# State products in column tiles, words scaled on VectorE, a row-tiled selection, and new durations for the planner

## The chip, the cores and the metric

One core of a Trainium2 chip runs the whole program. The metric is the device time of one execution in microseconds (us), the median of the runs shown. The engines are named as in the profile: PE (TensorE matmul), PEld (its weight load), DVE (VectorE), ACT (ScalarE), POOL (GpSimd) and SP (SyncE, which issues nearly all transfers in one queue).

## The reference, cut to what matters

```python
# 1. gated linear attention, B=4 H=8 S=768 D=48
scale = np.minimum(mag, 0.999) / (mag + 1e-06)            # mag = |a_re + i a_im|
for t in range(S):
    S_re, S_im = ar*S_re - ai*S_im + k_t v_t, ar*S_im + ai*S_re
    y[:, :, t] = einsum('bhd,bhde->bhe', q[:, :, t], S_re)
x = y.transpose(0, 2, 1, 3).reshape(3072, 384)
# 2. soft mixture of experts: 32 slots, 8 experts, 384 -> 1024 -> 384
d = softmax(x @ phi, axis=0);  slot_input = d.T @ x
slot_out[e] = relu(slot_input[e] @ w1[e]) @ w2[e]
x = softmax(x @ phi, axis=1) @ slot_out
# 3. feed-forward, 384 -> 2048 -> 384
g = np.maximum(0.01 * h, h)                               # h = x @ w_in
return g @ w_out
```

The arrays `w_in` and `w_out` of the feed-forward reach the kernel as 64-bit floats, which it turns into 32-bit floats itself.

## The kernel before, in words

**Attention.** The sequence is cut into 6 chunks of 128 steps, and each chunk into two units of 16 heads, so there are 12 units u = 0 to 11, of 128 x 768 values each. For a unit, `prep1`, `modulus`, `excess`, `logs` and `prep2` take the logarithm and the angle of the gates; `phase` and `decay` sum them along time with a triangular matmul (L562); `prep3` makes cosine and sine; `prep4` scales q and k (L619) and spreads them over the two (L628). Then `attend` works in four groups of four heads: `mA` transposes q and k (L643, copied out at L647 or L649), `mB` multiplies them (L658) and masks the result (L661, DVE), `mC` makes the output (L683), `mD` makes the state for the next chunk, and `mE` transposes the output (L721, L725, L728). The state product of `mD` (L700) takes, for each of 8 heads of a half unit, a 128 x 96 weight (k times cosine and sine) and 48 columns of v; it is made for the first ten units, two halves each, so 20 times. Its result is added to the old state and decayed (L710, L712, L713). After every second unit `slots` adds the chunk to the 32 slots of the mixture.

**64-bit words.** `narrow` turns 128 x 384 words of 64 bits into 32-bit floats: `ACT` takes the absolute value of the high words (L439), DVE bounds it from below (L440), shifts the mantissa (L441), puts in the sign (L442) and the low bits (L443). `conv_wi` does so for 16 pieces of `w_in` during attention, and `conv_wo` for 16 pieces of `w_out` around the start of the feed-forward, where it also splits the result in two (L471, L472).

**Experts and feed-forward.** `layer1` and `layer2` multiply the 32 slots with all expert weights: 64 slabs of 384 KB each, which stream in as buffers come free (`load_slabs`). `output` transposes the result, and `product` multiplies it with `w_in` (L1014). One 128-row tile holds four groups of 32 rows there; each group is picked out by a 128 x 128 matrix of zeros and ones, `sel`, which `select` builds, and lands in a tile `gs` (L1022, L1023). From there on `ffn1` (L1039, then L1041 to L1043) and `ffn2` (L1056 to L1058, 1152 matmuls of 384 columns in all) fill the rest of the program, and L1066 stores the output.

**What sets the order.** Nothing is issued as it is written. Every operation is given to `Plan` with an estimated duration; `Plan.emit` computes from these how late each may start (`backward`) and then fills each engine in turn (`forward`), taking the time at which a loaded tile is there from `delay`. The order that results is fixed in the program: each engine, and the transfer queue of SP, goes through its own list and waits at an instruction until what it needs is there. Buffers come from pools (`Tag`); the largest, `w`, has 33 tiles of 384 KB that gates, q, k, v, raw words and slabs share. The durations are numbers in the code, for example:

```python
pe(1.36, mm, ks + [v], [b])                        # mD, L702
cost = max(0.45, 0.06 + nbytes / 0.36e6)           # a transfer of SP, L110
return 0.0 if not o.bytes else 4.0 if o.eng == "POOL" else 2.0   # delay, L144
```

Of the kernel before, what the change touches and what calls it, by code (L numbers as in the profile page):

```python
# [42 lines left out]
EARLY, LATE = {9: 2, 10: 4, 11: 8}, (18,)  # L43
# [53 lines left out]
class Plan:  # L97
# [222 lines left out]
def tile_kernel(  # L320
# [316 lines left out]
    def mA(u, hq):  # L637
        for nm, tg in (("q", t_qt), ("k", t_kt)):
# [13 lines left out]
    def mB(u, hq):  # L652
        b, t = b_sc(), t_sc([P, 4, P])
# [10 lines left out]
    def mC(u):  # L664

# [68 lines left out]
    def slots(c):  # L734

        nonlocal phi_mm, ms_mm
        last = c == NCH - 1
# [429 lines left out]
```

## Time and profile before

| | |
|---|---|
| median of 3 runs | 502.66 us (502.05 to 502.67) |
| profiled execution | 502.35 us, span 500.6 us |
| instructions | 10447 |
| busy: PE, PEld, DVE, ACT, POOL | 485.2, 440.0, 318.6, 356.5, 18.2 us |
| chain of work that ended last | PE 70%, DVE 15%, ACT 8%, DMA 5% |
| moved by DMA | 67.09 MB, mean 134 GB/s |

The span runs from the first to the last instruction of the program; 1.75 us of the execution lie around it. The busy time of PE is an upper bound of its work, since matmuls overlap. A mean over the whole span hides that the program has stages: attention to about 234 us, the expert layers to about 274 us, and the feed-forward to the end. So the windows, which give busy time by stretch, are read beside the chain. In the rows, a 32-bit matmul counts as two instructions.

### The profile page before, as it was taken

Reading aid. Unit: us, or ns where it says so; the run is one execution under the profiler, and the core shown is the slowest. Engines: PE = TensorE matmul, PEld = TensorE weight load, DVE = VectorE, ACT = ScalarE, POOL = GpSimd, SP = SyncE. Lnnn points to the kernel's source line nnn. Section 1 sums busy time; section 2 is a strip of 40 time slices with the busy share of each in tenths; the row PEclk is TensorE's granted clock in tenths of the full one; section 3 lists DMA queues with packets and bytes.
Section 4 is the critical chain, followed back from the end, with each engine's and each line's share of the span. In section 5 each row is a group of like instructions: output and inputs, shape, how many; then the busy total and the mean of one; then the engine's idle time right before and its main releaser. Section 6 shows DMA issues by size and latency. Waiting matters only on the chain.

```text
span 500.6 us, 10447 instructions
## 1 busy us (share of the span) xinstructions
PE 485.2 (97%) x4066; PEld 440.0 (88%) x4066; DVE 318.6 (64%) x669; ACT 356.5 (71%) x684; POOL 18.2 (4%) x37
## 2 busy tenths in 40 slices
PE   8797999999999999999999999999999999999997
PEld 8675779979979988889545999999999999999996
DVE  3767899999999998986535999334500542035300
ACT  7998999999999999944215998079802993079502
POOL 1010002001001000001000000000000000000000
PEclk9999999999999999999999999999999999999999
DMA  8987344465677393599899221011000010010002
GB/s 300 324 196 234 98 129 147 109 192 142 181 221 217 75 260 118 191 323 318 286 395 352 64 64 33 0 48 48 2 0 33 17 48 1 0 48 16 33 1 94
DMA packets 46890, 67.09 MB, mean 134 GB/s; under 512 B 22004, under 2 KB 28132, under 8 KB 46840
## 3 DMA queue, kind: packets, MB, share of 16 engines
q1 hardware_dynamic: 46088, 65.99, 41.4%
q8 instruction: 32, 0.52, 0.4%
q10 hardware_dynamic: 432, 0.39, 0.2%
q0 software_dynamic: 320, 0.03, 0.1%
q14 instruction: 18, 0.15, 0.1%
HBM read 61.59 MB, written 4.81 MB: 133 GB/s over the span
## 4 chain that ended last, share of the span: by engine, by line
PE 70%; DVE 15%; ACT 8%; DMA 5%; issue 1%; SPq 0%; ACTq 0%; DVEq 0%
PE b L1056 13%; PE b L1058 13%; PE b L1057 13%; PE bm L683 5%; PE bsc L658 5%; PE b L1039 4%; PE btr L643 4%; PE bc L562 3%; PE bsc L700 3%; DMA w<-in_w_dram 2%; DVE w L619 2%; DVE sc L661 2%; DMA w<-in_wo_dram 2%; DVE q L628 2%; DVE k L628 1%; PE b L934 1%
## 5 line engine op out<-in xcount | busy, mean ns | idle before, releaser
L1043 DVE TENSOR_TENSOR w<-x,w 128x384 fp32r<-128x384 f32 x128 | 69.0, 555 | 104.6 <-ACT w L1042 103.8
L1056 PE MATMUL b<-w 128*128 128x384 f32 x384 | 128.5, 335 | 0.0
L1058 PE MATMUL b<-w 128*128 128x384 f32 x384 | 128.3, 334 | 0.0
L1057 PE MATMUL b<-w 128*128 128x384 f32 x384 | 128.3, 334 | 0.0
L1056 PEld LDWEIGHTS b<-w 128*128 128x128 f32 x384 | 72.1, 188 | 0.3 <-ACT x L1041 0.2
L1057 PEld LDWEIGHTS b<-w 128*128 128x128 f32 x384 | 72.1, 188 | 0.0
L1058 PEld LDWEIGHTS b<-w 128*128 128x128 f32 x384 | 72.1, 188 | 0.0
L1065 ACT ACTIVATE k<-b 128x384 f32<-128x384 f32 x24 | 11.4, 488 | 79.1 <-PE b L1058 78.9
L1042 ACT ACTIVATE w<-x 128x384 fp32r<-128x384 f32 x128 | 63.4, 525 | 4.9 <-PE b L1058 3.2
L1041 ACT ACTIVATE x<-b 128x384 f32<-128x384 f32 x128 | 59.9, 487 | 2.4 <-PE b L1039 1.5
L658 PE MATMUL bsc<-qt,kt 96*128 96x128 f32 x384 | 50.8, 278 | 0.4 <-DVE S L710 0.2
L658 PEld LDWEIGHTS bsc<-qt,kt 96*128 96x128 f32 x384 | 46.4, 192 | 2.1 <-DVE S L710 0.5
L661 DVE TENSOR_TENSOR sc<-bsc,tri_r 128x512 f32<-128x512 f32 x48 | 32.5, 684 | 7.3 <-PE bsc L658 6.9
L683 PE MATMUL bm<-sc,w 128*64 128x128 f32 (+1 forms) x384 | 35.5, 275 | 0.0
L649 ACT ACTIVATE qt<-btr 96x512 f32<-96x512 f32 x48 | 28.4, 591 | 9.2 <-PE btr L643 9.1
L186 ACT ACT_TABLE_LOAD x25 | 32.1, 1283 | 2.6 <-issue 2.2
L643 PE MATMUL btr<-ident,k 128*96 128x128 f32 x192 | 29.3, 275 | 2.4 <-ACT kt L649 1.7
L683 PE MATMUL bm<-qt,S 96*48 96x128 f32 x320 | 31.1, 272 | 0.0
L700 PEld LDWEIGHTS bsc<-w,k 128*96 128x96 f32 x320 | 28.9, 165 | 2.0 <-issue 1.0
L643 PE MATMUL btr<-ident,q 128*96 128x128 f32 x192 | 29.5, 276 | 1.2 <-DVE kt L647 0.6
L700 PE MATMUL bsc<-w,k 128*96 128x48 f32 x320 | 29.6, 247 | 0.3 <-PE bm L771 0.3
L643 PEld LDWEIGHTS btr<-ident,q 128*96 128x96 f32 x192 | 21.0, 127 | 6.2 <-issue 1.7
(179 smaller groups left out, 798.2 us busy)
## 6 DMA issues: line engine op xcount, KB each, us to landing
w<-in_w_dram SPq DMA_DIRECT2D x50, 384.0 KB, 6.1
w<-in_qkv_dram SPq DMA_DIRECT2D x36, 384.0 KB, 5.9
w<-in_a_dram SPq DMA_DIRECT2D x22, 384.0 KB, 4.2
w<-in_wi_dram SPq DMA_DIRECT2D x16, 384.0 KB, 4.2
w<-in_wo_dram SPq DMA_DIRECT2D x16, 384.0 KB, 5.5
out_dram<-k SPq DMA_DIRECT2D x24, 192.0 KB, 1.9
cs<-in_w_dram SPq DMA_DIRECT2D x4, 384.0 KB
k<-in_w_dram SPq DMA_DIRECT2D x6, 192.0 KB, 3.7
```

Source lines behind the costliest of these rows:

```text
L186: self.preload(TABLES[name])
L643: T.transpose(b()[:96, P * i:P * i + P], src()[:, i].rearrange("p t d -> p (t d)"), ident)
L658: T.matmul(b()[:, P * i:P * i + P], lhsT=k()[:96, i, :], rhs=q()[:96, i, :], start=True, stop=True)
L661: dve(c_dve(512), lambda: V.tensor_tensor(t(), b().rearrange("p (i t) -> p i t", t=P), tri.unsqueeze(1).to_broadcast([P, 4, P]), op=ALU.mu ...
L683: T.matmul(y()[64 * j:64 * j + m, o:o + P], lhsT=l, rhs=r, start=kind == 0, stop=kind == 1 or c == 0)
L700: T.matmul(b()[:96, D * i:D * i + D], lhsT=ks[i // 4]()[:, i % 4].rearrange("p t d -> p (t d)"), rhs=v()[:, D * g:D * g + D], start=True, ...
L1041: act(NG, lambda: A.activation(u(), b()[:, :NG], AF.Prelu, alpha=0.01), [b], [u])
L1042: act(NG, lambda: A.activation(g()[:, 0], u(), AF.Copy), [u], [(g, 0)])
L1043: dve(c_dve(NG), lambda: V.tensor_tensor(g()[:, 1], u(), g()[:, 0].bitcast(F32), op=ALU.subtract), [u, (g, 0)], [(g, 1)])
L1056: T.matmul(b()[:, :DM], lhsT=lh, rhs=wh()[:, i], start=f == FO[0], stop=False)
L1057: T.matmul(b()[:, :DM], lhsT=ll, rhs=wh()[:, i], start=False, stop=False)
L1058: T.matmul(b()[:, :DM], lhsT=lh, rhs=wl()[:, i], start=False, stop=f == FO[-1])
```

## The change

Four places of the work are changed, and numbers of the planner.

1. `mD`: each 128 x 96 weight is cut into three of 32 columns, which write to partitions 0, 32 and 64 of the output. There are 24 matmuls for 8.
2. `narrow`: the instruction on ACT and the bound are gone. DVE multiplies the high words by 2^-112 (it reads every second 32-bit word for that), shifts, and puts in sign and low bits as before; it has four instructions as before.
3. `select` and `product`: `sel` is one 128 x 128 tile for each half, built by 2 instructions in place of 5; the four groups are matmuls over 32 rows each.
4. `Plan`: durations in some twenty places, the time of a transfer, and the time until a large transfer has landed (4.0 us where it was 2.0). The order in which operations are given to the planner is written out as a string, `PROGRAM`; the same steps stand there in the same order as in the loop before. `LEADS` is empty.

```diff
-        act(n, lambda: A.activation(t1(), hi().bitcast(F32), AF.Abs), [raw], [k1])
-        dve(c_dve2(n), lambda: V.tensor_scalar(t1(), t1(), 2.0 ** -15, None, op0=ALU.max), [], [k1])
-        dve(c_dve2(n), lambda: V.tensor_scalar(i0(), i1(), 0x07FFFFFF, 3, op0=ALU.bitwise_and, op1=ALU.logical_shift_left), [k1], [k0])
-        dve(c_dve(n), lambda: V.scalar_tensor_tensor(i0(), hi(), -0x40000000, i0(), op0=ALU.bitwise_and, op1=ALU.bitwise_or), [raw], [k0])
+        dve(c_dve2(n), lambda: V.tensor_scalar(t1(), hi().bitcast(F32), 2.0 ** -112, None, op0=ALU.mult), [raw], [k1])
+        dve(c_dve2(n), lambda: V.tensor_scalar(i0(), i1(), 3, None, op0=ALU.logical_shift_left), [k1], [k0])
+        dve(c_dve(n), lambda: V.scalar_tensor_tensor(i0(), hi(), -0x80000000, i0(), op0=ALU.bitwise_and, op1=ALU.bitwise_or), [raw], [k0])
...
-                T.matmul(b()[:96, D * i:D * i + D], lhsT=ks[i // 4]()[:, i % 4].rearrange("p t d -> p (t d)"), rhs=v()[:, D * g:D * g + D], start=True, stop=True)
-
-        pe(1.36, mm, ks + [v], [b])
+                k = ks[i // 4]()[:, i % 4].rearrange("p t d -> p (t d)")
+                for x in range(0, 2 * D, 32):
+                    T.matmul(b()[x:x + 32, D * i:D * i + D], lhsT=k[:, x:x + 32], rhs=v()[:, D * g:D * g + D], start=True, stop=True)
+
+        pe(0.84, mm, ks + [v], [b])
...
-            sl = sel[h] = t_sc([P, 4, P], F32R)
-            dve(0.35, lambda sl=sl: V.tensor_scalar(sl(), stk.unsqueeze(1).to_broadcast([P, 4, P]), 0.0, None, op0=ALU.mult), ["stk"], [sl], after=[si])
-            for g in range(4):
-                half = lambda x, h=h: x.rearrange("p (m r s) -> p m r s", r=2, s=NSL)[:, :, h, :]
-                p = slice(32 * g, 32 * g + 32)
-                dve(0.1, lambda sl=sl, g=g, p=p, half=half: V.tensor_copy(half(sl()[p, g, :]), half(stk[p, :])), ["stk"], [sl])
+            sl = sel[h] = t_sc([P, P], F32R)
+            half = lambda x, h=h: x.rearrange("p (m r s) -> p m r s", r=2, s=NSL)[:, :, h, :]
+            dve(0.15, lambda sl=sl: V.tensor_scalar(sl(), stk, 0.0, None, op0=ALU.mult), ["stk"], [sl], after=[si])
+            dve(0.15, lambda sl=sl, half=half: V.tensor_copy(half(sl()), half(stk)), ["stk"], [sl])
...
-                    T.matmul(b2[g]()[:, y], lhsT=sel[0]()[:, g, :], rhs=h()[:, y], start=True, stop=False)
-                    T.matmul(b2[g]()[:, y], lhsT=sel[1]()[:, g, :], rhs=lo()[:, y], start=False, stop=True)
+                    p = slice(32 * g, 32 * g + 32)
+                    T.matmul(b2[g]()[:, y], lhsT=sel[0]()[p], rhs=h()[p, y], start=True, stop=False)
+                    T.matmul(b2[g]()[:, y], lhsT=sel[1]()[p], rhs=lo()[p, y], start=False, stop=True)
...
-            cost = max(0.45, 0.06 + nbytes / 0.36e6)
+            cost = max(0.45, nbytes / 0.4e6)
...
-        return 0.0 if not o.bytes else 4.0 if o.eng == "POOL" else 2.0
+        return 0.0 if not o.bytes else 4.0 if o.eng == "POOL" or o.bytes > 300000 else 2.0
...
-        pe(3.73 if c else 1.99, mm, ...
+        pe(3.7 if c else 1.92, mm, ...
-        phi_mm = pe(1.15, mm, ts + ["phi"], [b])
+        phi_mm = pe(1.01, mm, ts + ["phi"], [b])
```

The new numbers move instructions on every engine. Three places are shown; the names are those of the tiles. In the changed kernel the lines stand 11 to 14 further down: L523, L532, L549 and L585 are L512, L521, L538 and L574, L586 is L575, L630 is L619, L639 is L628, L659 is L647, L674 is L661, L573 is L562, L671 is L658, L717 is the state product L700, and L451 to L454 are the four DVE instructions of `narrow`.

DVE, from the third mask of unit 0 (`sc`) to the scaling of q and k of unit 1 (`w`, L619). Before:

```order
L661 TENSOR_TENSOR sc<-bsc,tri_r 128x512
L538 SCALAR_TENSOR_TENSOR w<-w 128x768
L661 TENSOR_TENSOR sc<-bsc,tri_r 128x512
L710 TENSOR_TENSOR S<-bsc,dc 96x384
L619 TENSOR_TENSOR w<-w 128x768
L628 TENSOR_TENSOR q<-w,cs 128x384
L619 TENSOR_TENSOR w<-w 128x768
L628 TENSOR_TENSOR q<-w,cs 128x384 x2
```

and now:

```order
L674 TENSOR_TENSOR sc<-bsc,tri_r 128x512
L451 TENSOR_SCALAR w<-w 128x384
L452 TENSOR_SCALAR w<-w 128x384
L453 SCALAR_TENSOR_TENSOR w<-w 128x384
L674 TENSOR_TENSOR sc<-bsc,tri_r 128x512
L451 TENSOR_SCALAR w<-w 128x384
L452 TENSOR_SCALAR w<-w 128x384
L451 TENSOR_SCALAR w<-w 128x384
L452 TENSOR_SCALAR w<-w 128x384
L454 SCALAR_TENSOR_TENSOR wi<-w 128x384
L453 SCALAR_TENSOR_TENSOR w<-w 128x384
L630 TENSOR_TENSOR w<-w 128x768 x2
```

Nine instructions of `narrow` stand here now, and five more follow before the last mask of unit 1; before, the first of them came behind the masks of unit 1.

SP, the queue at the same time (`wi` are raw words, `qkv` and `a` inputs of units, `dr` and `cr` the short transfers that carry a unit's last row on). Before:

```order
L580 DMA dr<-w 1x768
L609 DMA dc<-dr 48x16x1 x2
L583 DMA dr<-cr 128x6
L352 DMA w<-in_qkv_dram 128x768
L581 DMA cr<-dr 128x6
L488 DMA w<-in_a_dram 128x768 x2
L583 DMA dr<-cr 128x6
L352 DMA w<-in_qkv_dram 128x768
L488 DMA w<-in_a_dram 128x768 x2
L352 DMA w<-in_wi_dram 128x768
```

and now:

```order
L591 DMA dr<-w 1x768
L594 DMA dr<-cr 128x6
L364 DMA w<-in_qkv_dram 128x768
L364 DMA w<-in_wi_dram 128x768
L592 DMA cr<-dr 128x6
L364 DMA w<-in_wi_dram 128x768 x2
L856 DMA stk<-in_stk_dram 128x128
L594 DMA dr<-cr 128x6
L499 DMA w<-in_a_dram 128x768 x2
```

The first raw words are asked for ahead of the second `dr<-cr`, and three of them stand where one stood.

PE, around the first state product of unit 0 (`bsc<-w,k`). Before:

```order
L643 MATMUL btr<-ident,k 96x128 x4
L658 MATMUL bsc<-qt,kt 128x128 x8
L700 MATMUL bsc<-w,k 96x48 x8
L562 MATMUL bc<-w,tri_r 128x512
L562 MATMUL bc<-w,tri_r 128x256
```

and now:

```order
L671 MATMUL bsc<-qt,kt 128x128 x4
L573 MATMUL bc<-w,tri_r 128x512
L573 MATMUL bc<-w,tri_r 128x256
L671 MATMUL bsc<-qt,kt 128x128 x4
L717 MATMUL bsc<-w,k 32x48 x24
```

Twenty-four matmuls of 32 rows of output stand for eight of 96, and the sum over time of the next unit (`bc<-w,tri_r`) has moved ahead of them.

## Rows read from the trace of the kernel before

**Rows 1.** Windows: stretch in us; length, busy us (instructions) by engine, PEclk, DMA share, GB/s.

```profile
31.70:54.10 22.40, 18.30 (x167) 15.25 (x168) 14.61 (x24) 20.18 (x30) 1.88 (x3) 1.00 0.66 191
...
54.10:230.80 176.70, 175.02 (x1881) 153.13 (x1878) 169.61 (x325) 161.50 (x262) 11.53 (x19) 1.00 0.61 181
...
205.00:266.00 61.00, 60.21 (x762) 43.40 (x758) 38.37 (x113) 25.04 (x53) 3.19 (x8) 1.00 0.92 325
...
275.00:300.00 25.00, 25.00 (x145) 24.73 (x144) 24.93 (x59) 24.91 (x63) 0.00 (x0) 1.00 0.24 65
```

**Rows 2.** Timeline of DVE: start, length, instruction, [idle before it and what ended that].

```profile
31.00 0.68 DVE L661 TENSOR_TENSOR sc<-bsc,tri_r 128x512 f32<-128x512 f32 x1
...
35.62 0.96 DVE L619 TENSOR_TENSOR w<-w 128x768 f32<-128x768 f32 x1 [3.12 <-ACT w L602]
...
38.90 1.02 DVE L628 TENSOR_TENSOR k<-w,cs 128x384 f32<-128x384 f32 x2
...
53.38 0.69 DVE L661 TENSOR_TENSOR sc<-bsc,tri_r 128x512 f32<-128x512 f32 x1 [1.59 <-PE bsc L658]
...
229.49 1.28 DVE L661 TENSOR_TENSOR sc<-bsc,tri_r 128x512 f32<-128x512 f32 x2
```

**Rows 3.** Groups by line, 54.1 to 230.8 us (L439: to 213 us): count, busy us, mean ns.

```profile
L443 DVE SCALAR_TENSOR_TENSOR wi<-w 128x384 int32<-128x384 int32 x16 | 8.6, 550 | 0.1
...
L442 DVE SCALAR_TENSOR_TENSOR w<-w 128x384 int32<-128x384 int32 x16 | 8.3, 550 | 0.1
...
L440 DVE TENSOR_SCALAR w<-w 128x384 f32<-128x384 f32 x16 | 5.3, 350 | 0.9 <-ACT w L439 0.9
L441 DVE TENSOR_SCALAR w<-w 128x384 int32<-128x384 int32 x16 | 5.2, 354 | 0.2
...
L439 ACT ACTIVATE w<-w 128x384 f32<-128x384 f32 x16 | 8.5, 560 | 0.0
```

**Rows 4.** Chain of work that ended last, 145 to 176 us: start, length, piece.

```profile
149.61 1.32 PE bsc L700 x16
...
174.02 1.01 PE bm L745 x32
```

**Rows 5.** Timeline of PE and PEld in the second expert layer, 258.4 to 260 us.

```profile
258.53 0.49 PE L970 MATMUL b<-x,h 128*32 128x384 f32 x1
...
258.55 0.49 PE L970 MATMUL b<-w,h 128*32 128x384 f32 x2
...
258.85 0.49 PE L970 MATMUL b<-x,h 128*32 128x384 f32 x1
...
259.50 0.13 PEld L970 LDWEIGHTS b<-w,h 128*32 128x32 f32 x4 [0.19 <-issue]
```

**Rows 6.** Timeline of SP's queue, 24 to 34 us.

```profile
26.10 0.34 SPq L583 DMA_DIRECT2D dr<-cr  x1
...
33.21 0.43 SPq L352 DMA_DIRECT2D w<-in_wi_dram  x1
```

**Rows 7.** The page, DMA issues: transfer, count, KB each, median us to landing.

```profile
w<-in_wi_dram SPq DMA_DIRECT2D x16, 384.0 KB, 4.2
```

**Rows 8.** Waits of SP's queue, 188 to 210 us: us in total, times, longest.

```profile
SPq L352 <- DVE w L619: 7.6, 2, 5.5
SPq L352 <- DVE w L538: 5.3, 1, 5.3
SPq L352 <- PE bm L683: 5.0, 1, 5.0
```

**Rows 9.** Timeline of PE from the last expert slab to the feed-forward.

```profile
266.22 1.48 PE L970 MATMUL b<-w,h 128*32 128x384 f32 x10 [0.15 <-DMA w<-in_w_dram]
...
272.23 0.38 PE L1022 MATMUL b<-w,sc 128*128 128x256 f32 x1
...
273.48 0.28 PE L1022 MATMUL b<-w,sc 128*128 128x256 f32 x1
...
274.40 1.04 PE L1039 MATMUL b<-q,qt 128*128 128x384 f32 x5
```

More of the change, by code (lines that the diff above doesn't have):

```diff
@@ L42 @@
 ROUNDS = 6
-EARLY, LATE = {9: 2, 10: 4, 11: 8}, (18,)
+LATE = 18
+PROGRAM = """
+a0 a1 q0 P0 M0 X0 l0 P1 D0 A0 F0 A1 S0 a2 h a3 q1 G0 P2 M1 X1 l1 c0 a4 q2 F1 A2 S1 D1 G1 P3 M2 X2 l2
+c1 s0 k a5 q3 F2 A3 S2 D2 G2 P4 M3 X3 l3 c2 a6 q4 F3 A4 S3 D3 L0 G3 P5 M4 X4 l4 c3 c4 s1 a7 q5 F4 A5
+S4 D4 G4 P6 M5 X5 l5 c5 a8 q6 F5 A6 S5 D5 L1 G5 P7 M6 X6 l6 c6 s2 a9 q7 F6 A7 S6 D6 G6 P8 M7 X7 l7
+c7 a10 q8 F7 A8 S7 D7 L2 G7 P9 M8 X8 l8 c8 c9 s3 a11 q9 F8 A9 S8 D8 G8 P10 M9 X9 l9 c10 w2 q10 F9
+A10 S9 D9 L3 G9 P11 M10 X10 l10 c11 s4 w4 q11 F10 A11 S10 D10 G10 M11 X11 l11 c12 w8 F11 S11 D11 L4
+G11 c13 c14 c15 s5 L5
+"""
+LEADS = {k: float(v) for k, v in (x.split(":") for x in """
+""".split())}
 class Tag:
@@ L637, in mA @@
     def mA(u, hq):
+        plan.tag = f"a{u}.{hq}"
         for nm, tg in (("q", t_qt), ("k", t_kt)):
@@ L652, in mB @@
     def mB(u, hq):
+        plan.tag = f"b{u}.{hq}"
         b, t = b_sc(), t_sc([P, 4, P])
@@ L664, in mC @@
     def mC(u):
+        plan.tag = f"v{u}"
         c, bp = divmod(u, 2)
@@ L683, in mm @@
                             T.matmul(y()[64 * j:64 * j + m, o:o + P], lhsT=l, rhs=r, start=kind == 0, stop=kind == 1 or c == 0)
-        pe(3.73 if c else 1.99, mm, [x for hq in range(4) for x in (sc[u, hq], qt[u, hq, "q"])] + [v] + [(sbuf[bp], h) for h in range(2)], ys)
+        pe(3.7 if c else 1.92, mm, [x for hq in range(4) for x in (sc[u, hq], qt[u, hq, "q"])] + [v] + [(sbuf[bp], h) for h in range(2)], ys)
         for h in range(2):
@@ L689, in mD @@
     def mD(u, h):
+        plan.tag = f"d{u}.{h}"
         c, bp = divmod(u, 2)
@@ L715, in mE @@
     def mE(u, h):
+        plan.tag = f"e{u}.{h}"
         c, bp = divmod(u, 2)
@@ L736, in slots @@
         nonlocal phi_mm, ms_mm
+        plan.tag = f"s{c}"
         last = c == NCH - 1
@@ L771, in ms @@
                 T.matmul(b3()[32 * i:32 * i + 32, :DM], lhsT=dd()[:, NSL * i:NSL * i + NSL], rhs=xs[i](), start=True, stop=True)
-        ms_mm = pe(0.9, ms, [dd] + [k for x in xs for k in ((x, 0), (x, 1))], [b3])
+        ms_mm = pe(0.79, ms, [dd] + [k for x in xs for k in ((x, 0), (x, 1))], [b3])
         if c:
@@ L814, in step @@
                 turns.append((key, u))
-    def run(names, n=0):
-        for x in names.split():
-            step(x[0], n + int(x[1:]))
     def warm(n, b, after=()):
@@ L824, in tile_kernel @@
     warm(100, b_m())
-    run("a0 a1 q0 P0 M0 X0 l0 P1 D0 A0 F0 A1 S0 a2")
     nconv = 0
-    for n in range(NU):
-        load_slabs(EARLY.get(n, 0))
-        if n == 2:
-            plan.add("SP", 0, lambda: SY.dma_start(stk, stk_in), [], ["stk"], nbytes=65536)
-        if n == 0:
-            plan.add("SP", 0, lambda: SY.dma_start(phi, r_in), [], ["phi"], nbytes=57344)
-        run("a3 q1 F0 A1 S0 D0", n)
-        if n > 1 and n % 2 == 1:
-            turns.append(("L", n // 2 - 1))
-        prep4(n)
-        attend(n)
-        run("P2 M1 X1 l1", n)
-        for _ in range(3 if n == NU - 1 else 2 if n in (3, 7) else 1):
-            step("c", nconv)
-            nconv += 1
-        if n % 2:
-            slots(n // 2)
-    turns.append(("L", NCH - 1))
+    for word in PROGRAM.split():
+        key, n = word[0], int(word[1:] or 0)
+        plan.tag = word
+        if key in steps:
+            step(key, n)
+        elif key == "G":
+            prep4(n)
+            attend(n)
+        elif key == "s":
+            slots(n)
+        elif key == "L":
+            turns.append(("L", n))
+        elif key == "w":
+            load_slabs(n)
+        elif key == "h":
+            plan.add("SP", 0, lambda: SY.dma_start(phi, r_in), [], ["phi"], nbytes=57344)
+        elif key == "k":
+            plan.add("SP", 0, lambda: SY.dma_start(stk, stk_in), [], ["stk"], nbytes=65536)
+    plan.tag = ""
     for name in turns:
@@ L1038, in ffn1 @@
         w, o = gs[f // 4], P * (f % 4)
-        pe(0.17, lambda: T.matmul(b()[:, :NG], lhsT=w()[:, o:o + P], rhs=cT[j](), start=True, stop=True), [(w, o // 256), cT[j]], [b])
+        pe(0.1735, lambda: T.matmul(b()[:, :NG], lhsT=w()[:, o:o + P], rhs=cT[j](), start=True, stop=True), [(w, o // 256), cT[j]], [b])
         u, g = t_x(), t_w([P, 2, NG], F32R)
```

28 lines of the change are left out of this document (14 added, 14 removed).

## The prediction, made before the changed kernel had run

> **What bounds the kernel now.** I read the page first (its chain gives PE 70%, DVE 15%), then the windows, since the program has stages, and then the timelines at the seams. The feed-forward is PE alone: in its first 25 us PE issues 145 matmuls and is never idle, while DVE and ACT are just as full [rows 1]. Nothing in the change gives PE less to do there, so this stage keeps its length, and all that counts is when it begins.
>
> Attention is the stage that the change works on. I cut it at three masks on DVE: the last of unit 0 ends at 31.7 us, the last of unit 1 at 54.1 (53.38 + 0.69), the last of unit 11 at 230.8 (229.49 + 1.28) [rows 2]. Between the last two PE is busy for 175.0 of 176.7 us, DVE for 169.6, ACT for 161.5 [rows 1]. Three engines are nearly full at once. Taking work from one of them alone would leave the others; the stretch shrinks by about what the least relieved engine loses. Before it, from 31.7 to 54.1 us, DVE is busy for 14.6 of 22.4 us, so 7.8 are free [rows 1], 3.1 of them in one piece ahead of unit 1's scaling and 1.6 ahead of its last mask [rows 2].
>
> Behind attention the slabs bound: from 205 to 266 us the DMA engines are 92% busy [rows 1]. That burst begins when SP's queue, which stands still before 206 us, gets buffers that DVE (L619, L538) and PE (L683) of units 9 and 10 give back [rows 8]. So I take the burst to move with attention, and the feed-forward with the burst. The last slab's matmuls start at 266.2 us, the feed-forward's first matmuls behind the L1039 row of 274.4 [rows 9].
>
> **The change, part by part.**
>
> *State products, PE.* Now one takes 1.32 us for its 16 instructions [rows 4]. What would three column tiles of 32 take? The second expert layer runs four such tiles at once: a round of four starts within 0.02 us, the next 0.32 us later, for 384 columns, which is 0.83 ns a column and round [rows 5]. Four weight loads of 32 columns take 0.13 us together [rows 5]. Here a round has 48 columns, 0.040 us, and there are 16 rounds (8 heads, two instructions each): 0.64 us. L745 shows what comes on top: 8 rounds of 128 columns would be 0.85 us and take 1.01 [rows 4], 0.16 more for the run. So 0.80 us. The diff itself plans 0.84; in the same diff L745 goes from 1.15 to 1.01, which is the trace's value, so I take 0.84 and a saving of 0.48 us. The bounds are 0.64 (tiles overlap fully, no start) and 1.52 (each of 48 pairs at L745's pace, 1.01/32 = 31.6 ns). By the order, 17 of the 20 products stand between unit 1's and unit 11's output on PE: PE loses 17 x 0.48 = 8.2 us there.
>
> *Words, ACT.* L439 goes: 16 times 0.560 us, 8.5 us busy during attention [rows 3]; less the overlap of neighbours ACT loses some 7 us. The other 16, for `w_out`, fall beside a PE that is full, so they gain nothing; if PE were not full, they would.
>
> *Words, DVE.* There are four instructions before and after, of the same kinds: two like L440 and L441 (350 and 354 ns), two like L442 and L443 (550) [rows 3]. The new first one reads every second word. L442 and L443 do so too, but no one-input instruction here does. Its cost lies between 350 ns and the 550 of those two; I take 350, because the two-input kind costs no more strided than other 384-column instructions do. At the other end DVE loses 0.2 x 12 = 2.4 us of its gain in attention.
>
> So DVE's work is not less, but the order moves it. Between the last masks of unit 1 and unit 11 DVE had all 64 instructions of `narrow` and now has 50; fourteen come before. By kind they are 4, 4, 4 and 2: 4 x 0.350 + 4 x 0.354 + 6 x 0.550 = 6.1 us. Neighbours overlap by 0.08 (two of 0.55 take 1.02 [rows 2]), so 6.1 - 14 x 0.08 = 5.0 us. The cover is the 7.8 free us ahead: nine of them, 3.3 us, stand just where DVE waited 3.1 us for ACT. If that cover is gone, unit 1 ends up to 5.0 us later and nothing is won. For the cover the raw words must be there. SP asked for the first at 33.2; now it does so two places behind the first `dr<-cr`, which was issued at 26.1 [rows 6], so at about 27; with 4.2 us to landing [rows 7] they are there at 31, where the first of the nine would begin.
>
> *Selection and product.* `select` has fewer instructions, in free time of DVE. The second batch of 16 selecting matmuls runs from 273.48 to 274.40, 0.92 us [rows 9]. With 32-row groups that start in order, the second of one group can run beside the first of the next; I estimate 0.5 us from their pace of 0.115 (five steps for eight). So 0.4 us earlier; bounds 0 and 0.7 (four at once).
>
> *Planner.* The written-out order is the old one. New durations and landing times reorder every engine; of that I cost the fourteen instructions, and the rest at nothing, from minus 1 to plus 1.
>
> **Sum.** In the stretch PE loses 8.2, ACT about 7, DVE 5.0. The least is DVE's: 5.0. With 0.4 at the product that is 5.4. From the profiled execution, 502.35 us (0.3 below the median of the runs), it gives **497.0 us**.
>
> **The rivals.**
>
> *PE paces alone (more gain).* The chain names PE in most of attention and PE is the fullest of the three [rows 1]. If DVE's free 7 us are used up by the new order, the stretch shrinks by PE's 8.2: 502.35 - 8.2 - 0.4 = 493.7. Against it: 169.6 of 176.7 us leave DVE hardly more slack than PE has.
>
> *The burst does not follow.* SP waits for DVE's L619 of unit 10 for up to 5.5 us [rows 8]. By the order DVE has 265 instructions between unit 1's last mask and that one, 52 of them of `narrow`; now 262, of which 50. That is a relief of only about 1.1 us (three instructions). If it is this that lets the burst begin, 502.35 - 1.1 - 0.4 = 500.85.
>
> *The words come late.* DVE, not ACT, now stands at the first word of a piece, and unit 1's scaling stands behind it on DVE. At 27 plus 4.2 us there is no room to spare. Then the 5.0 are paid again ahead: 501.95.
>
> *The tiles do not pay (slower).* If the pairs of load and matmul of the small tiles follow one another at L745's 31.6 ns, one product takes 1.52 us, 0.20 more, 17 times: PE, the fullest engine, has 3.4 us more to do and sets the pace: 502.35 + 3.4 - 0.4 = 505.35. It decides from 1.32/48 = 27.5 ns a pair on. Against it speaks that four tiles start within 0.02 us [rows 5]; for it, that nothing in this trace runs pairs faster than 31.6 ns for long.
>
> *A floor for each matmul.* The same mechanism with a pace between: at 25 ns a pair one product would take 1.20 us, 0.12 less, PE would lose 17 x 0.12 = 2.0 and set the pace at 502.35 - 2.0 - 0.4 = 499.95. The Trainium skill has such a rule (TensorE: Matmul & The Clock Gate, "Wait — 56ns, not 53.3ns?"): starts never lie closer than about 25 ns, however few columns. The trace agrees only for one tile at a time: starts in different tiles lie closer than that [rows 5].
>
> **How the numbers follow.** Forecast 0.46; PE paces 0.17; the burst does not follow 0.14; words late 0.08; tiles do not pay 0.08; the floor 0.03; another mishap of the new order, slower, 0.04. About 0.2% (1 us) is what a measurement of this kernel tells from no change. Faster by more: 0.46 + 0.17 + 0.14 + 0.03 = 0.80; within: 0.08; slower: 0.12. The range leaves out those 0.20: its upper end, 501.2, takes in the burst that does not follow with the product's bound of 0; its lower, 491.9, lies halfway between PE's 493.7 and 490.1, where products of 0.64 us would put that case. The likeliest case's own range is 495.7 to 499.4, by the strided 2.4 us, the product's 0.3 and the planner's 1.
>
> **What would show it.** The state product should take 0.8 to 0.9 us in the chain; the first DVE instruction of `narrow` 350 ns; DVE should be over 85% busy from unit 0's to unit 1's last mask, with unit 1's at 54 us still; unit 11's last mask should come near 226 us, the last slab near 261, and the feed-forward should keep its length. The forecast is wrong if a state product takes over 1.2 us, if DVE waits for raw words in the first 60 us, or if the last mask moves and the last slab does not.

## The result, and the profile of the changed kernel

The changed kernel takes 496.31 us (median of 4 runs, 495.57 to 499.23) beside 502.67 us for the kernel before (4 runs, 502.05 to 504.29): a ratio of 0.9878, 95% interval 0.9838 to 0.9918. Its profiled execution took 496.04 us, the span is 494.3; forecast were 497.0. Run again on another chip it took 498.94 us (7 runs, 496.76 to 499.85), a ratio of 0.9926, interval 0.9896 to 0.9955; that difference is a finding of its own, below.

The windows of the changed kernel, columns as in [rows 1]: unit 0's to unit 1's last mask, unit 1's to unit 11's, the burst, and the feed-forward's first 25 us.

```profile
36.60:55.90 19.30, 14.18 (x195) 11.45 (x189) 19.06 (x36) 18.05 (x28) 1.30 (x2) 1.00 0.69 189
55.90:224.70 168.80, 167.00 (x2434) 142.29 (x2433) 164.80 (x313) 152.91 (x245) 10.67 (x19) 1.00 0.62 187
205.00:262.00 57.00, 54.88 (x702) 38.78 (x693) 31.00 (x94) 21.26 (x46) 2.96 (x8) 1.00 0.89 314
268.50:293.50 25.00, 24.77 (x142) 24.46 (x142) 25.00 (x61) 23.36 (x57) 0.00 (x0) 1.00 0.23 65
```

Read the second line against its counterpart in [rows 1]. The stretch fell from 176.7 to 168.8 us, by 7.9. PE's work fell by 8.0 (175.0 to 167.0), DVE's by 4.8 (169.6 to 164.8), ACT's by 8.6. PE is idle for 1.8 us of it, as before (1.7); DVE, which had 7.1 us free, has 4.0. So the stretch followed PE, and DVE gave up idle time. In the first line DVE is busy for 19.06 of 19.30 us: the words fill what was free there. That stretch is also 3.1 us shorter than before, since unit 0 now ends at 36.6 us instead of 31.7.

The pieces of the chain of work that ended last, from 100 to 176 us (start, length, piece), have the state product:

```profile
102.78 1.01 PE bm L764 x32
110.47 0.81 PE bsc L717 x48
112.29 0.81 PE bsc L717 x48
```

48 instructions in 0.81 us took the place of 16 in 1.32 [rows 4]; L764, untouched, still takes 1.01. The groups of DVE from 55.9 to 224.7 us, as in [rows 3], have the words:

```profile
L454 DVE SCALAR_TENSOR_TENSOR wi<-w 128x384 int32<-128x384 int32 x14 | 7.5, 550 | 0.1
...
L453 DVE SCALAR_TENSOR_TENSOR w<-w 128x384 int32<-128x384 int32 x12 | 6.6, 550 | 0.1
L451 DVE TENSOR_SCALAR w<-w 128x384 f32<-128x384 f32 x12 | 4.1, 350 | 0.0
L452 DVE TENSOR_SCALAR w<-w 128x384 int32<-128x384 int32 x12 | 4.1, 354 | 0.2
```

L451 reads every second word and costs 350 ns, like its dense forerunner; and 50 instructions are left in the stretch, as counted. DVE's timeline (columns as in [rows 2]) has the first word, the last mask of unit 1, and unit 11's:

```profile
34.63 0.36 DVE L451 TENSOR_SCALAR w<-w 128x384 f32<-128x384 f32 x1 [1.16 <-DMA w<-in_wi_dram]
...
55.22 0.68 DVE L674 TENSOR_TENSOR sc<-bsc,tri_r 128x512 f32<-128x512 f32 x1
...
224.00 0.69 DVE L674 TENSOR_TENSOR sc<-bsc,tri_r 128x512 f32<-128x512 f32 x1
```

Unit 1 ended at 55.90 instead of 54.07 us, 1.8 later. From the last slab to the feed-forward (PE's timeline, as in [rows 9]):

```profile
259.02 2.13 PE L983 MATMUL b<-w,h 128*32 128x384 f32 x16
...
267.38 0.40 PE L1036 MATMUL b<-w,sc 32*128 32x256 f32 x4
...
267.83 0.79 PE L1053 MATMUL b<-q,qt 128*128 128x384 f32 x3
268.50 0.41 PE L1070 MATMUL b<-w 128*128 128x384 f32 x1
```

The last slab is done at 261.15 us, 6.6 before its old time of 267.7, so the burst moved with attention. The second selecting batch lasts 0.45 us (267.38 to 267.83) where it lasted 0.92 [rows 9]. The feed-forward starts at 268.50 instead of 275.32 and its last matmul starts 221.9 us later, before 221.5.

The books, against the profiled execution of 502.35 us: unit 1 ends later, +1.8; the stretch is shorter, -7.9; from unit 11's mask to the feed-forward it is 43.8 us where it was 44.5, -0.7; the feed-forward is longer, +0.4. That makes -6.4; the two executions differ by 6.3.

### The profile page after: what moved, and what is told of

Read it like the earlier page. It is cut to its first block, busy times and chain, and to the rows that moved or that the text cites. A ratio compares the mean times of both kernels' runs of the same rounds, so it can differ in the third digit from the quotient of the medians.

```text
span 494.3 us, 11701 instructions
## 1 busy us (share of the span) xinstructions
PE 474.8 (96%) x4706; PEld 427.0 (86%) x4706; DVE 316.1 (64%) x663; ACT 340.4 (69%) x652; POOL 17.3 (4%) x37
## 4 chain that ended last, share of the span: by engine, by line
PE 80%; ACT 6%; DMA 6%; DVE 5%; issue 1%; SPq 1%; POOL 0%; ACTq 0%; DVEq 0%
PE b L1071 14%; PE b L1072 13%; PE b L1070 13%; PE bm L697 7%; PE bsc L671 7%; PE btr L655 7%; PE b L1053 4%; PE bc L573 4%; PE bsc L717 2%; PE b L983 2%; DMA w<-in_wo_dram 2%; PE bm L743 1%; DMA dr<-w 1%; ACT L198 1%; DMA w<-in_wi_dram 1%
## 5 line engine op out<-in xcount | busy, mean ns | idle before, releaser
L1057 DVE TENSOR_TENSOR w<-x,w 128x384 fp32r<-128x384 f32 x128 | 68.0, 554 | 106.8 <-ACT w L1056 106.8
L671 PE MATMUL bsc<-qt,kt 96*128 96x128 f32 x384 | 51.5, 280 | 1.3 <-DVE sc L674 0.6
L671 PEld LDWEIGHTS bsc<-qt,kt 96*128 96x128 f32 x384 | 47.2, 194 | 3.0 <-ACT kt L661 1.2
L674 DVE TENSOR_TENSOR sc<-bsc,tri_r 128x512 f32<-128x512 f32 x48 | 32.6, 685 | 3.6 <-PE bsc L671 3.3
L661 ACT ACTIVATE qt<-btr 96x512 f32<-96x512 f32 x48 | 28.0, 589 | 2.3 <-PE btr L655 2.3
L1053 PE MATMUL b<-q,qt 128*128 128x384 f32 x80 | 26.2, 337 | 0.5 <-ACT qt L1043 0.5
L639 DVE TENSOR_TENSOR q<-w,cs 128x384 f32<-128x384 f32 x48 | 25.9, 548 | 0.0
```

The lines of the kernel that those rows point to most:

```text
L671: T.matmul(b()[:, P * i:P * i + P], lhsT=k()[:96, i, :], rhs=q()[:96, i, :], start=True, stop=True)
L674: dve(c_dve(512), lambda: V.tensor_tensor(t(), b().rearrange("p (i t) -> p i t", t=P), tri.unsqueeze(1).to_broadcast([P, 4, P]), op=ALU.mu ...
L1053: pe(0.1735, lambda: T.matmul(b()[:, :NG], lhsT=w()[:, o:o + P], rhs=cT[j](), start=True, stop=True), [(w, o // 256), cT[j]], [b])
L1057: dve(c_dve(NG), lambda: V.tensor_tensor(g()[:, 1], u(), g()[:, 0].bitcast(F32), op=ALU.subtract), [u, (g, 0)], [(g, 1)])
```

## The experiments

Each compares with runs of the kernel before on the same chip (medians there 501.7 to 503.1 us). "Stretch" is the time from unit 1's to unit 11's last mask.

### Which part pays: tiles, words, order

**Tiles in the old order.** To the kernel before, only this:

```diff
-                T.matmul(b()[:96, D * i:D * i + D], lhsT=ks[i // 4]()[:, i % 4]..., rhs=v()[...], ...)
+                k = ks[i // 4]()[:, i % 4].rearrange("p t d -> p (t d)")
+                for x in range(0, 2 * D, 32):
+                    T.matmul(b()[x:x + 32, D * i:D * i + D], lhsT=k[:, x:x + 32], rhs=v()[...], ...)
```

> The kernel before with the state products in column tiles and nothing else; the planner is still told 1.36 us, so every engine keeps the order of before. In the changed kernel a product's first and last matmul start 0.67 us apart, before 1.23. Theory PE paces: 17 products in the stretch from unit 1's to unit 11's last mask give about 17 x 0.6 = 10 us of PE's time back and most of it is seen: 493 to 496 us. Theory DVE paces (my prediction's): DVE has its work in the old order, so no more than 1 or 2 us are seen: 500.5 to 502.

**Whole products in the new order.** The reverse edit in the changed kernel, its order kept:

> The changed kernel with the state products whole again (8 matmuls of 128 x 96 weights); the planner is still told 0.84 us, so every engine keeps the order of the changed kernel. Theory PE paces: 20 x 0.6 = 12 us come back, most of it seen: 504 to 508 us, as slow as before or slower. Theory DVE paces: the order with 14 instructions moved ahead holds the gain, 497 to 499 us.

**Words alone.** The same reverse edit, but planned at 1.36 us, so that the order is made for it (`pe(0.84, mm, ks + [v], [b])` becomes `pe(1.36, ...)`):

> The changed kernel with the state product whole again and planned at 1.36 us, so that the order is made for it: the reliefs of VectorE and ScalarE without PE's. Theory (three engines are nearly full from unit 1 to unit 11, and each relief needs the other): PE is 175 us busy in that stretch as before, the stretch stays within 175.5 to 177.5 us, and the kernel takes 501 to 506 us, no gain. Rival (moved words and ScalarE's relief pay by themselves, and PE's tiles only add theirs): the stretch shrinks to 172 to 174 us, 498 to 500 us.

Measured: tiles in the old order 498.93 us (498.31 to 500.42, 6 runs), ratio 0.9926 [0.9898, 0.9955]; whole products in the new order 505.77 (504.42 to 507.42, 11 runs), 1.0060 [1.0038, 1.0082]; words alone 505.39 (503.14 to 509.67, 12 runs), 1.0061 [1.0034, 1.0087]. The window of the stretch in each, columns as in [rows 1]; first tiles in the old order:

```profile
51.90:227.60 175.70, 168.78 (x2424) 141.55 (x2422) 168.99 (x325) 160.79 (x263) 13.49 (x19) 1.00 0.62 181
```

whole products in the new order:

```profile
57.80:234.40 176.60, 174.91 (x1894) 153.43 (x1894) 165.77 (x313) 153.62 (x245) 12.34 (x19) 1.00 0.61 178
```

and words alone:

```profile
62.60:237.50 174.90, 173.58 (x1892) 153.48 (x1892) 164.41 (x311) 152.83 (x247) 11.96 (x21) 1.00 0.61 182
```

Look at PE's idle time, length less busy. With tiles alone PE had 6.2 us less to do, but idled 6.9 us instead of 1.7: 175.7 us, hardly a gain there. (This execution is 4.0 us faster than before; 2.2 of that lie ahead of unit 1's end, which came at 51.9 us.) Its time fell between the ranges of the two theories. With whole products PE idles 1.7 and 1.3 us and sets the pace at its full work: 176.6 and 174.9; for the new order that is what "PE paces" had forecast. Only both together give 168.8. One thing is not shown: the tiles ran alone only in the order that was planned for 1.36 us, so how much of the 6.9 us belongs to that order stays open.

In the stretch the parts don't add: 1.0 for the tiles, 0.1 and 1.8 for the rest, 7.9 for all. Ahead of it they do something else: unit 1 ended at 51.9 us with tiles in the old order, at 57.8 and 62.6 in the two others, where it was 54.1. Unit 1's end in one execution carries some 3 us of chance in the new orders, as shown below; the stretch doesn't. Words alone are no gain, as the first theory had it, with a stretch 0.6 below its bounds; the profile is of the slowest of those 12 runs, so its 62.6 us is a late case.

**ScalarE's relief taken back.** The instructions that the change removed from ACT are put back as work whose result nobody reads, planned at no cost, so that the other engines keep their order. Ahead of the first DVE instruction of `narrow`, for `w_in`:

```diff
+        for _ in range(2 if idle else 0):
+            act(-114, lambda: A.activation(logits[:, 16:24, :]..., hi()[:, :256].bitcast(F32), AF.Abs), [raw], [])
```

> The changed kernel with two absolute values of 256 words each on ACT for each of the 16 pieces of w_in, planned as costing nothing and read by nobody; every other instruction keeps its place. ACT gets back some 0.7 us a piece, 8 to 11 us in attention. If ACT paces the stretch now, the time grows by over 5 us, to 502 or more; if it has room (152.9 us busy of 168.8), by 0 to 3 us, 496.3 to 499.

**Words late.** DVE converts the first four pieces only behind unit 1's last mask:

```diff
-c1 s0 k a5 q3 F2 ...
+c0 c1 s0 k a5 q3 F2 ...
-        conv(wi_in, i, lambda tmp: ...)
+        conv(wi_in, i, lambda tmp: ..., [masks[1, 3]] if i < 4 else ())
```

> The changed kernel, but the first four pieces of raw words may be converted on DVE only after the last mask of unit 1, so that the fourteen instructions stand behind it as before the change; planned anew. Theory of the prediction (DVE paces the stretch, and those instructions were moved into free time): the stretch from unit 1's to unit 11's last mask grows by about 5 us to 173 or 174, unit 1's mask comes up to 2 us earlier than 55.9, the kernel takes 498.5 to 500 us. Theory that DVE had idle time left in the stretch anyway and PE paces: the stretch stays at 169 us, the kernel takes 494.5 to 496.5.

Measured: with ACT's work back 505.47 us (505.14 to 505.92, 6 runs), ratio 1.0078 [1.0055, 1.0100]; with the words late 500.70 (496.88 to 501.97, 12 runs), 0.9966 [0.9941, 0.9992]. The stretch with ACT's work back:

```profile
59.30:233.60 174.30, 169.32 (x2431) 141.78 (x2433) 165.58 (x313) 161.07 (x268) 9.43 (x19) 1.00 0.60 180
```

and with the words late:

```profile
59.00:229.30 170.30, 166.34 (x2433) 142.35 (x2433) 168.25 (x327) 152.94 (x247) 11.97 (x20) 1.00 0.60 181
```

ACT's 8.2 us more cost 5.5 of the stretch, in this order, although ACT was busy for only 161.1 of 174.3 us: over 502 us, as forecast for an ACT that paces. ACT waited for no raw word in it; PE's waits for ACT rose from 1.7 to 4.7 us. The 14 instructions, whose move my whole sum was built on, are worth 1.5 in the stretch: without it DVE is busy for 168.25 of 170.3 us, and PE still idles only 4.0. That is near the theory in which PE paces (169), but the time is above both forecasts. The larger relief was the one I had put aside as not the least. Unit 1 ended at 59.0 with the words late; what held it there was something else, as shown below, so this run does not tell what the words cost ahead of unit 1.

**Old words, and old numbers.** The changed kernel with the four old instructions and ACT's Abs in `narrow`, planned anew; and the kernel before with the new work (tiles, words, selection), but the planner's other durations and landing times as they were.

> The changed kernel with the four-plus-one instructions of the old word conversion (absolute value on ACT, then four on DVE), planned anew with the new numbers. If the moved conversions made the gain (DVE paces), this loses about 5 us: 500 to 502. If PE paces and ACT and DVE have room, it loses 0 to 2 us: 496 to 498. Unit 0's last mask should be earlier than the changed kernel's 36.6 us if the raw words on DVE are what made it late.

> All three changes of the work (column tiles planned at 0.84 us, words without ACT, selection in row tiles), but the planner's other durations and landing times as before. If the gain is in the work, 494 to 498 us; if the new numbers carry part of it, 498 to 502 us. By the theory that early raw words behind longer landing times made units 0 and 1 late, unit 1's last mask comes nearer to 54 us than the changed kernel's 55.9.

Measured: 512.32 us (509.34 to 515.23, 6 runs), 1.0191 [1.0153, 1.0229], and 500.35 us (498.55 to 502.69, 12 runs), 0.9944 [0.9925, 0.9964]. The old words make a stretch of 185.3 us in which the clock is 0.97; the order that the planner makes for them is bad in its own way (unit 2 alone took 24.9 us), so this run prices an order more than the words, and I draw nothing else from it. The stretch with the old numbers:

```profile
55.90:225.80 169.90, 166.90 (x2436) 142.34 (x2436) 167.33 (x321) 154.20 (x247) 13.25 (x21) 1.00 0.65 192
```

Of the stretch's gain of 7.9 us, 6.8 are in the work and 1.1 in the numbers. The median lies where "the new numbers carry part of it" had been forecast; the runs spread by 4 us, so the time does not settle that share. Unit 1 ended at 55.9 us, no nearer to 54: that theory failed.

### Why unit 1 is late, and not by the same amount each time

In the changed kernel PE's waits from 20 to 56 us are (total, times, longest):

```profile
PE btr L655 <- ACT qt L661: 4.2, 3, 2.7
PE bc L573 <- DVE w L549: 1.5, 1, 1.5
PE bc L573 <- DMA w<-dr: 1.5, 1, 1.5
```

The longest, 2.7 us, is ahead of 24.5 us: the new order puts a table load and unit 2's first logarithm on ACT ahead of the copies of unit 0's first q and k. The third is for the accumulating transfer of unit 2's carried row, 3 KB, which POOL issues.

**Dummy matmuls in the first wait**, and **in four waits.** Both add matmuls whose results nobody reads behind transposes that are there; the order of everything else stays.

```diff
+                for _ in range(fill.get((u, hq, nm), 0)):
+                    T.matmul(b()[96:128, :P], lhsT=ident[:, 96:128], rhs=ident, start=True, stop=True)
...
+    fill = {(0, 0, "k"): 10, (1, 0, "k"): 2, (1, 1, "k"): 5, (1, 2, "q"): 7}
```

The first run has only the 10. With the other three entries goes the second.

> The changed kernel with ten small matmuls, read by nobody, on PE behind the first transposes of k of unit 0, in the 2.7 us in which PE waited for ACT at 22 to 24.5 us; every other instruction keeps its place. If the granted clock of 0.66 at 25 to 30 us came from that idle stretch and made unit 0 late, the clock there is 1.00, unit 0's last mask comes 1 to 2 us before 36.6, and the kernel takes 494.5 to 496. If the raw words and the carried rows alone made it late, nothing changes: 496 to 497.

> The changed kernel with 24 extra matmuls of 128 columns on PE, put behind the transposes that are already ahead of its early waits: 10 behind the first pair of unit 0 (PE stands 2.7 us there), and 2, 5 and 7 in unit 1, ahead of waits of 0.4, 1.1 and 1.5 us. Their results are read by nobody; the order of all other work is as in the changed kernel. Theory (PE's short idle stretches ahead of 50 us cost a drop of the granted clock, which makes unit 1 late): granted clock 1.00 in every slice from 20 to 60 us, end of unit 1's last mask 54.5 to 55.9 us, kernel 494.5 to 496.5 us, and a smaller range of the runs. Rival (unit 1 waits for VectorE and for the landing of the words, and the clock of PE there doesn't matter): mask at 55.9 to 58.7 us as without them, kernel 496 to 499 us.

**The changed kernel again**, beside the second of these:

> The changed kernel itself, beside two variants on one chip. Expected 496.3 us, 495.5 to 499.3. If its spread is the granted clock of the first 60 us (theory), its fast and its late runs differ in the whole by about 3 us and by the end of unit 1 (55.9 against 58.7 us) and in nothing behind it; if the spread is noise of the machine (rival), the milestones are shifted evenly.

Measured: 10 dummies 498.19 us (496.56 to 499.24, 6 runs), 0.9925 [0.9896, 0.9953]; 24 dummies 497.66 (496.44 to 501.52, 9 runs), 0.9909 [0.9878, 0.9939]; the kernel itself 498.94, 0.9926. Its second profile took 499.78 us. Here are its two windows, unit 0's to unit 1's mask and the stretch:

```profile
36.60:59.00 22.40, 17.67 (x205) 14.29 (x201) 19.35 (x37) 18.52 (x27) 1.61 (x2) 0.85 0.58 165
59.00:227.80 168.80, 167.01 (x2432) 142.29 (x2433) 164.84 (x313) 152.97 (x246) 12.08 (x19) 1.00 0.63 187
```

Unit 0 ends at 36.6 us in both executions and the stretch is 168.8 in both; of the 3.7 us between the two executions 3.1 arise between 36.6 and 59.0, and the rest at the seam to the feed-forward, which starts at 272.24. So the difference between the two has a place, nearly all of it where the theory had it. What differs there? The timeline of the second execution:

```profile
34.92 0.20 POOL L593 TENSOR_SCALAR cr<-cr 128x6 f32<-128x6 f32 x1 [6.68 <-DMA cr<-dr]
...
35.44 0.93 POOL L560 DMA_DIRECT2D w<-dr  x1 [0.31 <-ACT cs L601]
...
41.70 2.90 PE L573 MATMUL bc<-w,tri_p 128*128 128x512 f32 x4 [2.79 <-DMA w<-dr]
```

and of the first:

```profile
34.87 0.21 POOL L593 TENSOR_SCALAR cr<-cr 128x6 f32<-128x6 f32 x1 [6.55 <-DMA cr<-dr]
35.38 0.93 POOL L560 DMA_DIRECT2D w<-dr  x1 [0.30 <-ACT cs L602]
...
39.83 1.53 PE L573 MATMUL bc<-w,tri_p 128*128 128x512 f32 x4 [1.53 <-DMA w<-dr]
```

The transfer was issued at the same time, but PE could start 1.87 us later, after 2.79 us of waiting instead of 1.53; and then the same four matmuls took 2.90 us instead of 1.53. The granted clock from 40 to 45 us is 0.60 there (below) and 1.00 in the first: partly at the lower level, 1.2 GHz. Here a late landing of 3 KB cost its delay, and PE was slower behind it. The windows of the second execution:

```profile
25.00:30.00 5.00, 4.87 (x23) 4.39 (x22) 3.19 (x4) 2.99 (x5) 0.61 (x1) 0.50 0.87 230
40.00:45.00 5.00, 3.30 (x7) 1.96 (x8) 4.31 (x8) 1.61 (x4) 0.00 (x0) 0.60 0.69 262
45.00:50.00 5.00, 4.38 (x27) 3.82 (x25) 3.06 (x5) 4.57 (x8) 0.00 (x0) 0.72 0.44 84
```

of the run with 10 dummies:

```profile
25.00:30.00 5.00, 4.42 (x41) 4.20 (x39) 3.97 (x6) 4.89 (x9) 0.32 (x1) 1.00 0.97 236
...
45.00:50.00 5.00, 2.63 (x7) 1.34 (x8) 5.00 (x10) 4.97 (x8) 0.65 (x1) 0.66 0.62 157
```

and of that with 24:

```profile
25.00:30.00 5.00, 4.45 (x40) 4.45 (x41) 4.22 (x6) 4.87 (x10) 0.69 (x1) 1.00 0.85 196
...
45.00:50.00 5.00, 5.00 (x36) 3.83 (x35) 5.00 (x10) 4.97 (x8) 0.94 (x1) 1.00 0.59 158
```

The dummies do keep the clock up: at 25 to 30 us it is 1.00 instead of 0.50 or 0.66, and with 24 of them it stays so to 60 us, as forecast. But the 10 left a drop at 45 us; they brought unit 0's last mask forward by 0.9 us (1 to 2 were forecast), and the time lay above both forecasts. Compare the two runs in PE's sums for unit 2, in the four matmuls near 48 us and in unit 1's masks on DVE; first 10 dummies:

```profile
37.94 1.53 PE L573 MATMUL bc<-w,tri_p 128*128 128x512 f32 x4 [0.69 <-ACT w L521]
...
48.02 2.93 PE L573 MATMUL bc<-w,tri_r 128*128 128x512 f32 x4 [1.54 <-DVE w L549]
...
54.02 0.69 DVE L676 TENSOR_TENSOR sc<-bsc,tri_r 128x512 f32<-128x512 f32 x1 [2.59 <-PE bsc L673]
...
58.02 0.68 DVE L676 TENSOR_TENSOR sc<-bsc,tri_r 128x512 f32<-128x512 f32 x1
```

then 24:

```profile
37.54 1.53 PE L573 MATMUL bc<-w,tri_p 128*128 128x512 f32 x4 [0.46 <-DMA w<-dr]
...
47.80 1.56 PE L573 MATMUL bc<-w,tri_r 128*128 128x512 f32 x4
...
55.16 0.68 DVE L678 TENSOR_TENSOR sc<-bsc,tri_r 128x512 f32<-128x512 f32 x1
```

Two limits show. With 24 dummies PE starts the sums 2.29 us earlier than in the first execution of the changed kernel (37.54, there 39.83), and yet unit 1 ends at 55.84, there at 55.90. So at a full clock the sums don't hold unit 1. DVE does, by its timeline: in the first execution it has 0.24 us left of 19.30, with the words in it. With 10 dummies no landing was late either, and at 48 us PE is within 0.22 us of the run with 24; from there on it is at the lower clock (0.66 from 45 to 55 us), DVE waits 2.59 us for it, and unit 1 ends 2.9 us later, at 58.70. So a low clock can hold unit 1 by itself. In the changed kernel's second execution and in the run with the words late both came, a wait of 2.8 us for the landing and a clock of 0.60 and 0.58 from 40 to 45 us: 59.0 in both.

For the time it brought little: 497.66 us lies in the rival's range, and the range of the runs did not get smaller. The slower runs with 24 dummies (498.76 to 501.52 us) have a mean clock of 0.992 to 0.997, the faster ones 0.999 to 1.000, so the clock fell in those too; where, has no trace.

**Copies first.** Unit 2's logarithms on ACT are made to wait for the copies of unit 0's first q and k; the order is planned anew:

```diff
-            table(("P", u), "E", n, ..., AF.Ln), [(re, o)], [(lr, o)])
+            table(("P", u), "E", n, ..., AF.Ln), [(re, o)], [(lr, o)], copies if u == 2 else ())
```

> The changed kernel with one more rule for the planner: the logarithm of unit 2 on ACT stands behind the first copies of q and k of unit 0, as it did before the change; planned anew. If ACT's new order made PE wait 2.7 us and lose its clock, unit 0's last mask comes 2 to 4 us before 36.6, unit 1's 1 to 2 us before 55.9, the kernel takes 494 to 496 us. If the new plan is worse elsewhere, 496 to 499.

Measured: 498.91 us (496.51 to 499.64, 9 runs), 0.9945 [0.9926, 0.9964]: the forecast gain over the changed kernel did not come. Unit 0 ended at 31.9 us instead of 36.6, but unit 1 at 55.5. The timeline says what gave it back:

```profile
35.20 0.20 POOL L595 TENSOR_SCALAR cr<-cr 128x6 f32<-128x6 f32 x1 [7.71 <-DMA cr<-dr]
35.71 0.93 POOL L562 DMA_DIRECT2D w<-dr  x1 [0.31 <-issue]
...
40.70 2.90 PE L575 MATMUL bc<-w,tri_p 128*128 128x512 f32 x4 [3.73 <-DMA w<-dr]
```

ACT's arctangent, the other thing that the accumulating transfer needs, had ended at 32.2 us. The transfer was issued at 35.71, since on POOL's queue a multiplication for *unit 1's* carried row stood ahead of it, which is for unit 3, and which waited 7.7 us for its own transfer. PE then waited 3.73 us, and its clock was 0.50 from 40 to 45 us.

**The transfer ahead of the multiplication.** On top of copies first; PE, DVE and ACT keep their order.

In `emit`, with `mul` and `acc` POOL's multiplications and accumulating transfers as planned:

```diff
+        m = mul[1]
+        back = [x for x in m.outs if row.index(x) < row.index(acc[0])]
+        best[1][:] = [y for x in best[1] if x[1] is not m and x[1] not in back for y in ([x] + [(None, z) for z in [m] + back] if x[1] is acc[0] else [x])]
```

> The variant with unit 0's first copies ahead of unit 2's logarithms (copies_first), and on POOL's queue the accumulating transfer of unit 2's carried row moved ahead of the multiplication for unit 1's carried row (and SP's write of that product moved behind it); all other orders as in copies_first. There the multiplication waited 7.7 us for its DMA and started at 35.20 us, the transfer behind it was issued at 35.71 although its arctangent had ended at 32.2, PE waited 3.73 us for its landing and started at 40.70, at a clock of 0.50. Theory (the wait of PE ahead of unit 2's phase sums, which makes unit 1 late in every version with the new order, is a queue behind a waiting instruction on POOL): the transfer is issued at 32.3 to 32.8 us, PE's sums start at 37.0 to 38.0, the clock stays 1.00 to 40 us, unit 1's last mask ends at 52.5 to 53.8 us instead of 55.5, and the kernel takes 495.5 to 497.5 us (copies_first 498.9). Rival (the landing itself is late, behind bulk loads, whenever it is issued, or VectorE with its moved words holds unit 1): PE's sums start at 40 us or later, or unit 1 stays at 55 to 56 us, kernel 498 to 499.5 us.

Measured: 496.31 us (496.23 to 497.89, 6 runs), ratio 0.9883 [0.9848, 0.9918]. The timeline, with ACT's arctangent as its first line:

```profile
30.90 0.84 ACT L566 ACTIVATE w<-w 128x768 f32<-128x768 f32 x1
32.06 0.93 POOL L569 DMA_DIRECT2D w<-dr  x1 [4.88 <-ACT w L566]
35.12 0.42 POOL L602 TENSOR_SCALAR cr<-cr 128x6 f32<-128x6 f32 x1 [2.13 <-DMA cr<-dr]
...
37.93 1.53 PE L582 MATMUL bc<-w,tri_p 128*128 128x512 f32 x4 [1.45 <-DMA w<-dr]
```

The window of its stretch:

```profile
52.90:224.40 171.50, 167.04 (x2431) 142.27 (x2433) 166.97 (x317) 154.25 (x248) 10.98 (x19) 1.00 0.63 188
```

The theory's numbers came in, but for the issue at 32.06 us (32.3 to 32.8 forecast; this execution was half a microsecond ahead from unit 0 on): PE's sums at 37.93 us instead of 40.70, at full clock, unit 1 at 52.9 instead of 55.5, the stretch 171.5 us in both, the median 2.6 us lower. The two ran on different chips, but the intervals of their ratios do not meet. So in the order with copies first it was a queue behind a waiting instruction, on the engine that is least busy of all. Twelve of the fourteen word instructions stand ahead of unit 1's last mask here too, and it ends earlier than before the change (54.1): the words alone need not make unit 1 late.

In the changed kernel's own order POOL's queue is a smaller part. There the arctangent ended at 33.90 us,

```profile
33.06 0.84 ACT L557 ACTIVATE w<-w 128x768 f32<-128x768 f32 x1
```

and the transfer was issued at 35.38. In the run above the issue followed the arctangent by 0.32 us, so the queue cost at most 1.2 us, in the second execution 0.6. And an earlier start of the sums did not bring unit 1 forward there, as the run with 24 dummies showed. No run moves the transfer in that order alone.

This version is as fast as the changed kernel's better executions and 2.6 us faster than its second series, which ran on another chip; whether it beats the changed kernel on one chip was not tried. Its stretch is still 2.7 us longer than the 168.8 of the changed kernel; both together would be worth trying.

## Why the prediction was right, and where it was not

The time was forecast at 497.0 us and came out at 496.3 and 498.9. It is right by its terms for the work, and by luck: two misses of opposite sign, a stretch that shrank by 2.9 us more than the sum had and a unit 1 that ended 1.8 us late, nearly cancelled.

*State products.* Forecast 0.84 us, in the chain 0.81, from the pace of four tiles in another stage [rows 5]: 17 x (1.32 - 0.81) = 8.7 us, beside the 8.2 forecast and the 8.0 by which PE's work fell. The two rivals in which tiles pay little or nothing are out. 0.81/48 is 17 ns for a pair of load and matmul. The Trainium skill (TensorE: Matmul & The Clock Gate, "Wait — 56ns, not 53.3ns?") has starts no closer than about 25 ns; across three column tiles the trace does not agree. In one tile 16 pairs in 0.81 us are 51 ns each, which the rule allows.

*Words.* The strided instruction cost 350 ns, the value taken. DVE's work in the stretch fell by 4.8 us (forecast 5.0), ACT's by 8.6 (some 7).

*The rule that failed:* "the stretch shrinks by about what the least relieved engine loses". It gave 5.0 us; the stretch lost 7.9, PE's 8.0. That is the size of the rival "PE paces alone", and for its reason: DVE's idle time, which I took as fixed, went from 7.1 to 4.0 us. Against that rival I had held that DVE has "hardly more slack than PE"; by the same rows it had 7.1 us, and PE 1.7. But PE doesn't pace by itself. With PE's relief alone the stretch lost 1.0, and with ACT's taken back 5.5 of the 7.9 were gone. I had the bound of each engine and no account of how they wait for one another.

*Unit 1's mask unchanged at 54 us:* failed. It came at 55.9 and 59.0. I had put the danger at the raw words; DVE did wait for them, 1.16 us, which I had named as a sign against the forecast. The larger price came from what the planner's term had at nothing: ACT's new order let unit 0 end at 36.6 us instead of 31.7 (with copies first it was 31.9). The words then fell into a DVE that had no more room; by the timelines that gives the 55.9, though no run takes the words away while the clock stays full. A late landing and a lower clock give the 59.0. So the danger of the rival "the words come late" was there, by another road. In the first profiled execution 1.8 us of the stretch's surplus of 2.9 went there, in the second 4.9. With tiles alone in the old order, 498.93 us and ratio 0.9926, one is as well off as with the whole change in its second series: what the new order wins behind unit 1 it can lose ahead of it.

*Burst and seam.* The last slab was forecast near 261 us and ended at 261.15, so the rival in which the burst stays behind is out. Of the product's 0.4 us, 0.47 came (0.92 to 0.45). The feed-forward kept its length to 0.4 us.

## What to carry to other kernels

Where several engines are nearly full, look at the idle time of the fullest one in each version: here it stayed at 1.8 us (1.7 before) when all were relieved and rose to 6.9 when PE alone was, so the parts of such a change could not be priced one by one. When an order changes, read the first units as closely as the steady ones, and look for a waiting instruction at the head of every queue, the idlest engine's too. And profile the same kernel twice: what stayed equal to a tenth of a microsecond here was the kernel's own, and what moved pointed at a landing and at the clock.

## What the hardware showed that I had not expected

A transfer of 3 KB, issued at 35.4 us in two executions of the same kernel, released PE at 39.8 and at 41.7 us, while the DMA engines were 0.81 and 0.73 busy (35 to 40 us). The same four matmuls of 128x512 took 1.53 us at a granted clock of 1.00 and 2.90 after a wait of 2.79 us, in a stretch whose clock was 0.60. 0.50 is the lower level, 1.2 GHz: in the second execution the 5 us from 25 have it whole, behind a wait of 2.7 us. And the clock can fall without a late landing: with 10 and with 24 dummies the same sums (L573) began at 48.02 and 47.80 us and took 2.93 and 1.56 us.
